# A top-k attention and two gated expert layers on one core: the first batch in plain float32, score tiles copied out of PSUM

## The chip, the core and the metric

The kernel runs on one core of one Trainium2 chip. The metric is the device time of one execution in microseconds (us). The engines are TensorE (PE in the profile, its weight loads PEld), VectorE (DVE), ScalarE (ACT), GpSimd (POOL) and SyncE (SP), whose queue issues all of this kernel's DMAs. TensorE writes only PSUM, a memory of eight banks of 512 float32 columns; all else lies in SBUF.

## The reference

Attention over 4 batches, 8 heads, 576 positions and head size 64, in which each query keeps its 32 best scores, then two expert layers on the 2304 tokens:

```python
scores = scale * np.matmul(q, k.transpose(0, 1, 3, 2))
kth = np.partition(scores, -32, axis=-1)[..., -32:-31]
scores = np.where(scores >= kth, scores, -1e9)
attn = softmax(scores)                               # rows of 576
x = (attn @ v) as 2304 x 512                         # float32
h = x @ w_in;  g = where(h >= 1, h, where(h <= -1, 0, (h + 1)**2 / 4));  x = g @ w_out     # 512 -> 2048 -> 512
g = x @ w_gate;  out = (g * sigmoid(g) * (x @ w_val)) @ w_out2                             # 512 -> 1536 -> 512
```

The weights come in as 8-byte floats, and the attention scores must be near float32, since a wrong score changes which 32 are kept.

## The kernel before

**Arithmetic.** Nearly all matmuls take float32r, a 4-byte form of which one pass does not carry all float32 digits. So each operand is split into a high and a low part (`split`, `hilo`: ACT writes the high part, POOL subtracts for the low one), and a product is made of three or four matmuls. Transposes of the attention weights are plain float32 (`L747`, `L751`).

**Attention.** A unit is one batch, a pair of heads and a block of query tiles (two tiles of 128, or three of which the last holds 64 rows of each head). There are 8 units per batch, first block before second block, and 36 score tiles of 128 x 576 in each batch, 144 in all. For each score tile PE writes two half rows of 288 columns into one of two pairs of PSUM banks, `pS` (`L672`, four matmuls; each pair holds one score tile). DVE then works on it for some 6 us: four times MAX8 (`L686`), three times MATCH_REPLACE8 (`L696`) between them, and one SCALAR_TENSOR_TENSOR, the mask (`L700`), which compares the scores with the 32nd, multiplies with the exponentials that ACT has made (`L693`) and sums. The first MAX8, the first MATCH_REPLACE8, the exponential and the mask read the scores in PSUM, so a pair of banks comes free with the mask. Then PE transposes the masked tile (`L747`), ACT takes it out as high part (`L732`) and full copy (`L734`), POOL subtracts the low part (`L736`), PE multiplies with v (`L615`, `L617`), two ACT copies and two POOL operations add the parts and divide by the sum. In the 8 units of batch 0 (`LO_PE = 8`) the low part comes from PE instead: it subtracts the high part in PSUM with a matmul by a negative identity (`L725`), and ACT copies both parts (`L723`, `L727`).

**Preparing q, k, v.** Each is loaded per head pair, split by ACT and POOL (`L482`, `L484`), and q and k are transposed by PE and taken out by ACT (`L501`, `L537`).

**Weights.** 68 tiles of 8-byte weights are turned into high and low float32r by ACT (`L827`, `L830`, `L837`), DVE (`L832`) and POOL (`L835`, `L850`) and stored in DRAM. In the first 24, DVE's `L832` reads one operand in PSUM (a `pM` bank), in the other 44 both in SBUF.

**Expert layers.** `STEPS` goes through the tokens in subsets of 256 (the last one 512), first layer 1 (`L967`, `L1009`), then layer 2 (`L967`, `L1081`). Their sums lie in `pM`, two PSUM banks while attention runs; the other six are `pS` (four) and `pT` (two, transposes and attention outputs). When all attention is done, `pS` and `pT` pass to the experts (`p.heirs`).

**Order.** A planner (`Plan`) runs a list schedule forward and backward over all operations, with a price for each and the sizes of the rings of buffers, and writes one fixed order per engine. Each engine then does its instructions in that order, and waits at each for what it needs.

## Time and profile before

| what | value |
|---|---|
| median of 3 runs | 1330.06 us (1329.61 to 1332.45) |
| profiled execution, span from first to last instruction | 1326.2 us |
| busy: PE / DVE / ACT / POOL | 1208.5 / 1017.7 / 876.4 / 778.3 us |
| mean granted TensorE clock | 0.957 of full |

The profile is of one execution, and its page gives for that only the span; the median lies 3.9 us above it. In the page's 40 slices each digit is a tenth of busy time in 33 us. "Busy" of PE counts a matmul from its start to its modelled end, so neighbours overlap. The group rows give the mean duration of one instruction in ns, then the idle time of its engine just ahead of it and what ended that.

### The profile page before, as it was taken

How to read it: one execution, taken by the hardware profiler on the slowest of the kernel's cores; microseconds unless marked ns; L12 is line 12 of the kernel's file. 1: busy time of each engine (PE TensorE's matmuls, PEld its weight loads, DVE VectorE, ACT ScalarE, POOL GpSimd, SP SyncE). 2: the span in 40 equal slices, each digit the busy share in tenths (PEclk: the TensorE clock that was granted, in tenths of full speed). 3: DMA queues.
4: the chain of work that ended last, by engine and by line, in shares of the span. 5: the costliest groups of instructions: out<-in, count | busy, mean ns of one | idle time of the engine just before them, and what ended most of it. 6: DMA issues, size and time to landing. Idle time of an engine off the chain costs nothing.

```text
span 1326.2 us, 23321 instructions
## 1 busy us (share of the span) xinstructions
PE 1208.5 (91%) x7832; PEld 1095.6 (83%) x7832; DVE 1017.7 (77%) x2066; ACT 876.4 (66%) x1926; POOL 778.3 (59%) x831
## 2 busy tenths in 40 slices
PE   2556589888899999999999999999999999999998
PEld 2444489886799989998999988889999888888887
DVE  5899999899899989999999898989999312212212
ACT  6889799889777578776879777767766322333220
POOL 7888868689856465866667665556655313213210
PEclk9666699999899999999999999999999999999999
DMA  8788879789877786778676854548666754666452
GB/s 279 276 287 272 287 262 350 280 269 337 294 272 280 276 320 240 297 263 304 232 275 227 318 196 128 176 162 288 216 252 249 283 198 146 248 220 220 163 191 64
DMA packets 137032, 328.18 MB, mean 247 GB/s; under 512 B 21072, under 2 KB 66640, under 8 KB 136912
## 3 DMA queue, kind: packets, MB, share of 16 engines
q1 hardware_dynamic: 136912, 326.68, 70.2%
q8 instruction: 62, 1.02, 0.3%
q14 instruction: 58, 0.48, 0.1%
HBM read 282.07 MB, written 44.56 MB: 246 GB/s over the span
## 4 chain that ended last, share of the span: by engine, by line
PE 68%; DMA 9%; ACT 7%; DVE 7%; POOL 6%; issue 3%; SPq 0%; DVEq 0%; POOLq 0%; ACTq 0%
PE pM L967 25%; PE pM L1009 10%; PE pM L1081 7%; PE late L967 7%; PE pS L672 4%; PE pT L615 4%; PE late L1081 3%; PE pT L747 3%; DVE v L686 2%; PE late L1009 2%; DVE R L696 2%; POOL ct L835 2%; DMA cv<-in_moe_w_val_dram 2%; DMA cv<-in_moe_w_out_dram 1%; DMA w<-ws_moe_w_out 1%
## 5 line engine op out<-in xcount | busy, mean ns | idle before, releaser
L686 DVE MAX8 v<-R 128x8 f32<-128x576 f32 x432 | 315.1, 749 | 0.8
L967 PE MATMUL pM<-w,w 128*128 128x256 f32 (+1 forms) x1719 | 295.8, 319 | 3.5 <-DVE t L1105 2.5
L967 PEld LDWEIGHTS pM<-w,w 128*128 128x128 f32 x1719 | 249.9, 196 | 19.7 <-DVE t L1105 2.6
L736 POOL TENSOR_TENSOR PT<-F,PT 128x384 fp32r<-128x384 f32 (+2 forms) x192 | 176.7, 930 | 90.8 <-ACT F L734 84.4
L875 POOL TENSOR_TENSOR w<-t,w 128x512 fp32r<-128x512 f32 x110 | 142.2, 1295 | 135.1 <-ACT w L873 113.8
L696 DVE MATCH_REPLACE8 R<-v,R 128x576 f32<-128x576 f32 x288 | 213.8, 743 | 0.0
L686 DVE MAX8 v<-pS 128x8 f32<-128x576 f32 x144 | 109.3, 759 | 38.8 <-PE pS L672 36.3
L1009 PE MATMUL pM<-w,w 128*128 128x256 f32 (+1 forms) x867 | 132.2, 291 | 1.3 <-DVE t L1047 1.3
L693 ACT ACTIVATE E<-pS,nb 128x576 f32<-128x576 f32 x144 | 107.4, 746 | 25.3 <-DVE R L696 19.2
L747 PE MATMUL pT<-idf,E 128*128 128x128 f32 x512 | 95.9, 293 | 28.9 <-ACT qT L537 16.0
L1009 PEld LDWEIGHTS pM<-w,w 128*128 128x128 f32 x867 | 114.2, 190 | 4.0 <-DVE t L1047 2.7
L672 PE MATMUL pS<-kT,qT 128*128 128x288 f32 x512 | 100.9, 321 | 17.2 <-DVE E L700 14.9
L700 DVE SCALAR_TENSOR_TENSOR E<-pS,v,E 128x576 f32<-128x576 f32 x144 | 115.8, 804 | 0.2
L732 ACT ACTIVATE PT<-pT 128x384 fp32r<-128x384 f32 (+2 forms) x192 | 88.4, 463 | 40.6 <-PE pT L747 21.6
L696 DVE MATCH_REPLACE8 R<-v,pS 128x576 f32<-128x576 f32 x144 | 107.7, 748 | 0.0
L873 ACT ACTIVATE w<-t 128x512 fp32r<-128x512 f32 x110 | 70.5, 642 | 54.0 <-DVE t L1115 43.0
L835 POOL TENSOR_TENSOR ct<-ct,cv 128x512 int32<-128x512 int32 x68 | 91.4, 1348 | 22.9 <-ACT ct L830 15.1
L875 POOL TENSOR_TENSOR late<-t,late 128x512 fp32r<-128x512 f32 x32 | 41.3, 1293 | 103.8 <-ACT late L873 84.1
L747 PEld LDWEIGHTS pT<-idf,E 128*128 128x128 f32 x512 | 65.3, 148 | 42.6 <-ACT qT L537 18.1
L672 PEld LDWEIGHTS pS<-kT,qT 128*128 128x128 f32 x512 | 82.1, 206 | 22.3 <-DVE E L700 17.6
L967 PE MATMUL pM<-late,w 128*128 128x256 f32 (+1 forms) x597 | 98.5, 302 | 0.7 <-DVE t L1047 0.6
L615 PE MATMUL pT<-PT,v 128*128 128x256 f32 (+1 forms) x512 | 94.1, 310 | 3.9 <-ACT PT L727 3.1
(138 smaller groups left out, 2679.7 us busy)
## 6 DMA issues: line engine op xcount, KB each, us to landing
w<-ws_moe_w_out SPq DMA_DIRECT2D x134, 512.0 KB, 6.3
w<-ws_moe_w_in SPq DMA_DIRECT2D x90, 512.0 KB, 5.7
w<-ws_moe_w_val SPq DMA_DIRECT2D x55, 512.0 KB, 5.4
...
```

The source lines that it names most:

```text
L615: nc.tensor.matmul(av[:, 0:N], V[:, h, c, :], PT[:, s, h * 4 + c, 0:N], start=s == 0 and c == 0, stop=False)
L672: nc.tensor.matmul(ps[:, j, 0:288], l(), kT[:, hh, at + j * 288:at + (j + 1) * 288], start=k == 0, stop=k == len(lhs) - 1)
L686: p.op("DVE", self.dve(576) + (0 if k else self.PS), lambda: nc.vector.max(out=v8[:, h, k, :], in_=rr() if k else sc()), [Rb if k else ps] ...
L696: p.op("DVE", self.dve(576) + 0.06 + (0 if k else self.PS), lambda h=h, k=k, sc=sc, rr=rr: nc.vector.match_replace(out=rr(), in_to_replace ...
L700: p.op("DVE", self.dve(576) + 0.06 + self.PS, lambda h=h, sc=sc, ee=ee: nc.vector.scalar_tensor_tensor(out=ee(), in0=sc(), scalar=v8[:, h, ...
L736: p.op("POOL", self.pool(n), lambda: nc.gpsimd.tensor_tensor(out=dst(1), in0=src(F), in1=dst(0).bitcast(F32), op=OP.subtract), [F, (PT, (0 ...
L747: fn = (lambda ps=ps, m=m, h=h, c=c: nc.tensor.transpose(ps[:, m * 128:(m + 1) * 128], Sb[:, h, 64 * h + c * 128:64 * h + (c + 1) * 128], ...
L835: p.op("POOL", self.pool(512), lambda: nc.gpsimd.tensor_tensor(out=ci(), in0=ci(), in1=word(0), op=OP.add), [(cv, 0)], [ct], 3, tag + "cvadd")
L875: p.op("POOL", self.pool(n), lambda: nc.gpsimd.tensor_tensor(out=dst[:, 1, to:to + n], in0=src[:, off:off + n], in1=dst[:, 0, to:to + n].b ...
L967: nc.tensor.matmul(ps[:, at:at + n], W[:, w, k * 128:(k + 1) * 128], x[:, s, xat:xat + n], start=k == 0 and j == 0, stop=k == KC - 1 and j ...
L1009: nc.tensor.matmul(ps[:, at:at + n], WO[f][:, v, j * 128:(j + 1) * 128], g[:, s, gat:gat + n], start=q == 0 and m == 0, stop=q == 3 and m ...
L1081: nc.tensor.matmul(ps[:], a[:, s, at:at + 128], WO[f][:, v, :], start=q == 0 and m == 0, stop=q == 3 and m == 2)
```

## The change

Batch 0 is computed without splitting: `load_raw0` puts the two heads of a pair side by side, one transpose gives both stacked on 128 partitions, scores and outputs are plain float32 matmuls (`prep_k32`, `prep_q32`, `prep_v32`), and the attention weights are copied once. In all batches ACT copies each score tile from PSUM to SBUF (`C`, two buffers), and DVE and the exponential read `C`. `pS` shrinks to one pair of banks and `pM` grows from two banks to four. Buffers of batch 0 (`kF`, `vF`, `qF`, `PF`, `raw0`) pass on to the later batches (`chain`) in a fixed sequence. `E` has two buffers instead of three. A few prices of the planner change (`DMA_LAT`, ACT on converts and on copies across partitions, POOL), and switches that no longer choose anything go (`LO_W`, `QFIRST`, `AV_POOL`, `LATE`, `BANKS`). The core of the diff:

```diff
-    DMA_LAT = 1.7
+    DMA_LAT = 2.0
...
-    LO_PE = 8
+    FIRST_B = 1
...
-        self.r_v = R("v", [128, 2, 5, 2 * D], F32R, self.KV)
+        self.r_raw0 = R("raw0", [128, 5, 2 * D], F32, 2)
+        self.r_hl = R("hl", [128, 2, 5, 2 * D], F32R, 0)
+        self.r_v = R("v", [128, 2, 5, 2 * D], F32R, 0)
...
-        self.r_qT = R("qT", [128, 2, 2, 256], F32R, self.QT)
+        self.r_qT = R("qT", [128, 2, 2, 256], F32R, 0)
...
-        self.r_kT = R("kT", [128, 2, 640], F32R, self.KV)
-        self.r_E = R("E", [128, 2, S], F32, 3)
+        self.r_kT = R("kT", [128, 2, 640], F32R, 0)
+
+        self.r_kF = [R("kF%d" % i, [128, 2, 640], F32, 1) for i in range(HP)]
+        self.r_vF = [R("vF%d" % i, [128, 10, 128], F32, 1) for i in range(HP)]
+        self.r_qF = R("qF", [128, 512], F32, 2)
+        self.r_PF = R("PF", [128, 9, 320], F32, 2)
+        self.r_E = R("E", [128, 2, S], F32, 2)
...
-        self.r_PT = R("PT", [128, 2, 9, 320], F32R, 1)
+        self.r_PT = R("PT", [128, 2, 9, 320], F32R, 0)
...
-        self.p_s = R("pS", [128, 2, 512], F32, 2, "P")
+        self.p_s = R("pS", [128, 2, 512], F32, 1, "P")
+        self.r_C = R("C", [128, S], F32, 2)
         self.p_t = R("pT", [128, 512], F32, self.PT_BANKS, "P")
-        self.p_m = R("pM", [128, 512], F32, 4 - self.PT_BANKS, "P")
-
-        p.heirs = [((self.r_cv, self.r_ct), self.r_w, 5)] * self.LATE
-
-        p.heirs += [((self.p_s, self.p_t), self.p_m, 4 + self.PT_BANKS)] * self.BANKS
+        self.p_m = R("pM", [128, 512], F32, 6 - self.PT_BANKS, "P")
+
+        self.chain = []
+        for i in range(HP):
+            self.chain += [((self.r_kF[i],), self.r_kT, 1), ((self.r_vF[i],), self.r_v, 1)]
+        self.chain[-1:] = [((self.r_raw0,), self.r_hl, 1), ((self.r_qF,), self.r_qT, 1), self.chain[-1],
+                           ((self.r_PF,), self.r_PT, 1), ((self.r_cv, self.r_ct), self.r_w, 5)]
+        gone = ()
+        for own, ring, n in self.chain:
+            gone += own
+            p.heirs.append((gone, ring, n))
+        self.chain.append(((self.p_s, self.p_t), self.p_m, 2 + self.PT_BANKS))
+        p.heirs.append(self.chain[-1])
...
             self.p.rush = self.FIRST and u == 0
+            if b < self.FIRST_B:
+                if blk == 0:
+                    kF = self.prep_k32(b, hp)
+                state["q", u] = self.prep_q32(b, hp, self.BLOCKS[b][blk])
+                self.p.rush = False
+                if blk == 0:
+                    state["kv", b, hp] = kF, self.prep_v32(b, hp)
+                return
...
+    def load_raw0(self, src, b, hp, a=0, z=5):
+
+        raw = self.r_raw0.new()
+        m = min(z, 4)
+        for h in (0, 1):
+            d = slice(64 * h, 64 * h + 64)
+            if m > a:
+                self.dma(lambda d=d: raw[:, a:m, d],
+                         lambda h=h: src[b, 2 * hp + h, 0:512, :].rearrange("(p c) d -> p c d", c=4)[:, a:m, :],
+                         128 * 256 * (m - a), writes=[(raw, h)], prio=2, tag="ldqkv")
+            if z == 5:
+                self.dma(lambda d=d: raw[d, 4, d], lambda h=h: src[b, 2 * hp + h, 512:576, :],
+                         32 * 1024, writes=[(raw, 2 + h)], prio=2, tag="ldqkv")
+        return raw
+
+    def prep_k32(self, b, hp):
+
+        nc, p = self.nc, self.p
+        kF = self.r_kF[hp].new()
+        raw = self.load_raw0(self.t["k"], b, hp)
+        ps = self.p_t.new()
+        for c in range(4):
+            p.op("PE", 0.11, lambda c=c: nc.tensor.transpose(ps[:, c * 128:(c + 1) * 128], raw[:, c, :], self.idf),
+                 [raw], [(ps, c)], 1, "kTt")
+        p.op("ACT", self.act(512), lambda: nc.scalar.activation(
+            out=kF[:, 0, 0:512], in_=ps[:], func=AF.Copy), [ps], [(kF, 0)], 2, "kTe")
+        pl = self.p_t.new()
+        p.op("PE", 0.11, lambda: nc.tensor.transpose(pl[:, 0:128], raw[:, 4, :], self.idf), [raw], [pl], 1, "kTt")
+        for h, r in enumerate((slice(0, 64), slice(64, 128))):
+            p.op("ACT", self.act(64), lambda r=r: nc.scalar.activation(
+                out=kF[r, 0, 512:576], in_=pl[r, r], func=AF.Copy), [pl], [(kF, 1 + h)], 2, "kTe")
+        return kF
+
+    def prep_v32(self, b, hp):
+
+        p, t = self.p, self.t["v"]
+        vF = self.r_vF[hp].new()
+        nc = self.nc
+        p.op("DVE", self.dve(1280), lambda: nc.vector.memset(vF[:], 0.0), [], [vF], 1, "vz")
+        for h in (0, 1):
+            d = slice(64 * h, 64 * h + 64)
+            self.dma(lambda h=h, d=d: vF[:, 4 * h:4 * h + 4, d],
+                     lambda h=h: t[b, 2 * hp + h, 0:512, :].rearrange("(p c) d -> p c d", c=4),
+                     128 * 1024, writes=[(vF, h)], prio=2, tag="ldqkv")
+            self.dma(lambda d=d: vF[d, 8, d], lambda h=h: t[b, 2 * hp + h, 512:576, :],
+                     32 * 1024, writes=[(vF, 2 + h)], prio=2, tag="ldqkv")
+        return vF
+
+    def prep_q32(self, b, hp, qts):
+
+        nc, p = self.nc, self.p
+        raw = self.load_raw0(self.t["q"], b, hp, qts[0], qts[-1] + 1)
+        qF = self.r_qF.new()
+        ps = self.p_t.new()
+        n = len(qts) * 128
+        for i, c in enumerate(qts):
+            p.op("PE", 0.11, lambda i=i, c=c: nc.tensor.transpose(ps[:, i * 128:(i + 1) * 128], raw[:, c, :], self.idf),
+                 [raw], [(ps, i)], 1, "qTt")
+        p.op("ACT", self.act(n), lambda: nc.scalar.activation(
+            out=qF[:, 0:n], in_=ps[:, 0:n], func=AF.Copy), [ps], [qF], 2, "qTe")
+        return qF
...
+        plain = b < self.FIRST_B
+        if plain:
+            av = self.p_t.new()
+
+            def mms():
+                for s in range(9):
+                    nc.tensor.matmul(av[:, 0:N], V[:, s, :], PT[:, s, 0:N], start=s == 0, stop=s == 8)
+            p.op("PE", self.mm(4 * N, 9), mms, [V] + [(PT, (i, g)) for i, t in enumerate(qts) for g in ((0, 1, 2) if t < 4 else ("a", ("b", 0), ("b", 1)))], [av], 1, "av")
+            p.op("ACT", self.act(N), lambda: nc.scalar.activation(
+                out=y[:, 0:N], in_=av[:, 0:N], func=AF.Copy), [av], [y], 2, "ave")
+        else:
+            tmp = self.r_tmp.new()
...
+            if plain:
+                cols = slice(i * 128, (i + 1) * 128)
+                r = slice(64 * h, 64 * h + 64) if t < 4 else slice(0, 128)
+                parts = ((0, 0, 0, 288), (1, 0, 288, 576)) if t == 4 or h == 0 else ((0, 0, 512, 576), (0, 64, 0, 224), (1, 0, 224, 512))
+                rd = [q] + [(kT, e) for e in (0, 1, 2)]
...
+                if plain:
+                    mine = [x for x in parts if x[0] == j]
+
+                    def mms(ps=ps, mine=mine, r=r, cols=cols):
+                        for jj, at, a, z in mine:
+                            nc.tensor.matmul(ps[:, jj, at:at + z - a], q[r, cols], kT[r, 0, a:z], start=True, stop=True)
+                    p.op("PE", sum(self.mm(4 * (z - a)) for _, _, a, z in mine), mms, rd, [(ps, j)], 0, "qk")
+                    continue
...
-            def vmax(k, h=h, ps=ps, Rb=Rb, sc=sc, rr=rr):
-                p.op("DVE", self.dve(576) + (0 if k else self.PS), lambda: nc.vector.max(
-                    out=v8[:, h, k, :], in_=rr() if k else sc()), [Rb if k else ps], [(v8, (h, k))], 6, "max8")
+            Cb = self.r_C.new()
+
+            def cc(Cb=Cb):
+                return Cb[:].rearrange("p (j n) -> p j n", j=2)
+            p.op("ACT", self.act(576), lambda sc=sc, cc=cc: nc.scalar.activation(out=cc(), in_=sc(), func=AF.Copy), [ps], [Cb], 1, "scp")
+            def vmax(k, h=h, Cb=Cb, Rb=Rb, cc=cc, rr=rr):
+                p.op("DVE", self.dve(576), lambda: nc.vector.max(
+                    out=v8[:, h, k, :], in_=rr() if k else cc()), [Rb if k else Cb], [(v8, (h, k))], 6, "max8")
 
...
-            p.op("ACT", self.act(576, self.FN - self.SB), lambda h=h, sc=sc, ee=ee: nc.scalar.activation(
-                out=ee(), in_=sc(), func=AF.Exp, bias=nb[:, h:h + 1], scale=0.125), [ps, (nb, h)], [(Eb, h)], 1, "exp")
+            p.op("ACT", self.act(576, self.FN), lambda h=h, cc=cc, ee=ee: nc.scalar.activation(
+                out=ee(), in_=cc(), func=AF.Exp, bias=nb[:, h:h + 1], scale=0.125), [Cb, (nb, h)], [(Eb, h)], 1, "exp")
             for k in range(3):
-                p.op("DVE", self.dve(576) + 0.06 + (0 if k else self.PS), lambda h=h, k=k, sc=sc, rr=rr: nc.vector.match_replace(
-                    out=rr(), in_to_replace=v8[:, h, k, :], in_values=rr() if k else sc(), imm_value=NEG),
-                    ([] if k else [ps]) + [(v8, (h, k))], [Rb], 6, "mrep")
+                p.op("DVE", self.dve(576) + 0.06, lambda h=h, k=k, cc=cc, rr=rr: nc.vector.match_replace(
+                    out=rr(), in_to_replace=v8[:, h, k, :], in_values=rr() if k else cc(), imm_value=NEG),
+                    ([] if k else [Cb]) + [(v8, (h, k))], [Rb], 6, "mrep")
                 vmax(k + 1)
-            p.op("DVE", self.dve(576) + 0.06 + self.PS, lambda h=h, sc=sc, ee=ee: nc.vector.scalar_tensor_tensor(
-                out=ee(), in0=sc(), scalar=v8[:, h, 3, 7:8], in1=ee(),
+            p.op("DVE", self.dve(576) + 0.06, lambda h=h, cc=cc, ee=ee: nc.vector.scalar_tensor_tensor(
+                out=ee(), in0=cc(), scalar=v8[:, h, 3, 7:8], in1=ee(),
                 op0=OP.is_ge, op1=OP.mult, accum_out=rs[:, i, h:h + 1]),
-                [ps, (v8, (h, 3))], [(Eb, h), (rs, (i, h))], 5, "mask")
+                [Cb, (v8, (h, 3))], [(Eb, h), (rs, (i, h))], 5, "mask")
...
-            if lo_pe and key in range(3):
-
-                p.op("ACT", self.act(n), lambda: nc.scalar.activation(out=dst(0), in_=src(ps), func=AF.Copy),
-                     [ps], [(PT, (0, i, key))], 2, "PThi")
-                p.op("PE", self.mm(n), lambda: nc.tensor.matmul(
-                    src(ps), self.idn[:], dst(0), start=False, stop=True, skip_group_check=True), [(PT, (0, i, key))], [(ps, None)], 1, "PTn")
-                p.op("ACT", self.act(n), lambda: nc.scalar.activation(out=dst(1), in_=src(ps), func=AF.Copy),
-                     [ps], [(PT, (1, i, key))], 2, "PTlo")
+            if plain:
+                p.op("ACT", self.act(n), lambda: nc.scalar.activation(out=dst(None), in_=src(ps), func=AF.Copy),
+                     [ps], [(PT, (i, key))], 2, "PThi")
```

The places that matter below, as the engines' instruction orders have them. First ACT at the very start of the program, in which `cv` are loaded weights, `ct`, `w` and `pM` their converted pieces, `kT`/`kF` and `qF` the transposed keys and queries, and `C` the new copy; before:

```order
L482 ACTIVATE hq_190<-raw_184 128x2x2x64
L827 ACTIVATE pM_253<-cv_243 128x512
L482 ACTIVATE hl_185<-raw_183 128x10x64
L830 ACTIVATE ct_247<-cv_243 128x512
L827 ACTIVATE pM_254<-cv_244 128x512
L1196 ACTIVATE idn<-idf 128x128
L830 ACTIVATE ct_248<-cv_244 128x512
L827 ACTIVATE pM_253<-cv_245 128x512
L501 ACTIVATE kT_193<-pT_251 128x512
```

and now:

```order
L935 ACTIVATE ct_280<-cv_276 128x512
L932 ACTIVATE pM_288<-cv_277 128x512
L935 ACTIVATE ct_281<-cv_277 128x512
L558 ACTIVATE kF_220<-pT_285 128x512
L932 ACTIVATE pM_289<-cv_278 128x512
L563 ACTIVATE kF_220<-pT_286 64x64 x2
L942 ACTIVATE w_254<-ct_280 128x512
L592 ACTIVATE qF_228<-pT_285 128x256
L932 ACTIVATE pM_290<-cv_279 128x512
L942 ACTIVATE w_255<-ct_281 128x512
L935 ACTIVATE ct_280<-cv_278 128x512
L792 ACTIVATE C_283<-pS_282 128x576
```

The splits are gone, the first transposed keys are taken out at the sixth place of ACT's order (counted from its table load) instead of the tenth, and the first copy of a score tile stands behind the first step of four weight tiles' conversions.

Next PE at the end of attention: the last transposes of an attention tile (`E`), the expert matmuls around them (`pM<-`, 512 columns, three passes each), and the first attention outputs behind them; before:

```order
L747 MATMUL pT_252<-idf,E_198 128x128 x3
L747 MATMUL pT_251<-idf,E_198 128x128 x3
L967 MATMUL pM_254<-w_235,late_1_3206 128x512 x3
L967 MATMUL pM_253<-w_235,w_227 128x512 x3
L747 MATMUL pT_252<-idf,E_198 128x128 x2
L751 MATMUL pT_252<-idf,E_198 128x128
L967 MATMUL pM_254<-w_233,late_1_3206 128x512 x3
L967 MATMUL pM_253<-w_233,w_227 128x512 x3
L967 MATMUL pM_254<-w_234,late_1_3206 128x512 x3
L615 MATMUL pT_251<-PT_215,v_189 128x256 x4
```

and now:

```order
L1060 MATMUL pM_287<-w_265,w_267 128x512 x3
L1060 MATMUL pM_288<-w_268,late_2_2879 128x512 x3
L1060 MATMUL pM_288<-late_3_2880,late_2_2879 128x512 x3
L852 MATMUL pT_285<-idf,E_233 128x128 x2
L852 MATMUL pT_286<-idf,E_233 128x128 x2
L856 MATMUL pT_286<-idf,E_233 128x128
L1060 MATMUL pM_288<-w_262,late_2_2879 128x512 x3
L1060 MATMUL pM_288<-w_265,late_2_2879 128x512 x3
L1060 MATMUL pM_289<-w_268,w_259 128x512 x3
L1060 MATMUL pM_289<-late_3_2880,w_259 128x512 x3
L707 MATMUL pT_285<-late_0_2791,late_0_2786 128x256 x4
```

What moved is how far the experts have come at that point. Counted to the end of PE's order, 1242 expert matmuls of 512 columns stand behind the last transposes before (762 of `L967`, 192 of `L1009`, 288 of `L1081`), and 1194 now (714, 192 and 288); the 20 attention outputs and 2 transposes left are the same.

## Rows read from the trace of the kernel before

**Rows 1.** Page, 40 slices of 33 us: busy tenths, and granted clock.

```profile
PE   2556589888899999999999999999999999999998
DVE  5899999899899989999999898989999312212212
PEclk9666699999899999999999999999999999999999
```

**Rows 2.** Four stretches: length, busy us (instructions) of PE, PEld, DVE, ACT, POOL; clock, DMA.

```profile
0.00:166.00 166.00, 85.54 (x367) 67.52 (x368) 138.57 (x275) 136.82 (x281) 135.52 (x137) 0.70 0.82 280
166.00:400.00 234.00, 209.24 (x1542) 196.35 (x1541) 219.56 (x443) 199.98 (x443) 182.67 (x181) 0.97 0.84 294
400.00:1040.00 640.00, 631.73 (x4676) 598.24 (x4675) 596.29 (x1258) 467.33 (x1082) 395.74 (x463) 1.00 0.71 251
1040.00:1326.00 286.00, 281.99 (x1254) 233.48 (x1252) 63.32 (x92) 72.25 (x122) 64.35 (x52) 1.00 0.53 183
```

**Rows 3.** Waits of DVE, 33 to 1034 us: total us, times, longest us.

```profile
DVE v L686 <- PE pS L672: 36.3, 57, 1.8
DVE cv L832 <- ACT pM L827: 5.6, 6, 1.9
```

**Rows 4.** Timeline of the start: start us, us, engine, line, operation.

```profile
7.04 0.72 ACT L482 ACTIVATE hl<-raw 128x640 fp32r<-128x640 f32 x1
7.84 1.53 POOL L484 TENSOR_TENSOR hl<-raw,hl 128x640 fp32r<-128x640 f32 x1 [2.65 <-DVE cv L832]
...
9.43 1.26 PE L498 MATMUL pT<-idr,hl 128*128 128x128 f32 x8 [9.43 <-POOL hl L484]
...
18.26 0.76 DVE L686 MAX8 v<-pS 128x8 f32<-128x576 f32 x1
```

**Rows 5.** Groups by line and shape: busy us, mean ns, idle before.

```profile
L686 DVE MAX8 v<-R 128x8 f32<-128x576 f32 x432 | 315.1, 749 | 0.8
L696 DVE MATCH_REPLACE8 R<-v,R 128x576 f32<-128x576 f32 x288 | 213.8, 743 | 0.0
L700 DVE SCALAR_TENSOR_TENSOR E<-pS,v,E 128x576 f32<-128x576 f32 x144 | 115.8, 804 | 0.2
L686 DVE MAX8 v<-pS 128x8 f32<-128x576 f32 x144 | 109.3, 759 | 38.8 <-PE pS L672 36.3 <-PE pT L747 1.4 <-PE pT L544 0.5
L696 DVE MATCH_REPLACE8 R<-v,pS 128x576 f32<-128x576 f32 x144 | 107.7, 748 | 0.0
L832 DVE SCALAR_TENSOR_TENSOR cv<-cv 128x512 int32<-128x512 int32 x44 | 43.1, 980 | 4.5 <-ACT cv L827 3.0 <-issue 1.4
L887 ACT ACTIVATE t<-pM 128x512 f32<-128x512 f32 x50 | 30.1, 602 | 17.4 <-PE pM L1081 9.4 <-PE pM L1009 7.6
L725 PE MATMUL pT<-PT,idn 128*128 128x384 f32 x48 | 22.9, 488 | 13.5 <-ACT PT L723 13.5
L832 DVE SCALAR_TENSOR_TENSOR cv<-cv,pM 128x512 int32<-128x512 int32 x24 | 16.5, 685 | 22.0 <-ACT pM L827 21.1 <-issue 0.9
```

**Rows 6.** Line L832 with both operands in SBUF: duration ns min/median/max, first and last start.

```profile
L832 DVE SCALAR_TENSOR_TENSOR cv<-cv x44: 669/822/1798, 102.1 to 319.3; 128x512 int32<-128x512 int32 x44
```

**Rows 7.** The stretch of those 44, columns as in Rows 2.

```profile
102.00:320.00 218.00, 174.61 (x1173) 158.70 (x1173) 207.45 (x404) 190.77 (x417) 176.28 (x168) 0.88 0.84 292
```

**Rows 8.** Timeline around the last score tile's mask and the last transposes.

```profile
1032.85 0.81 DVE L700 SCALAR_TENSOR_TENSOR E<-pS,v,E 128x576 f32<-128x576 f32 x1
...
1037.49 0.27 PE L751 MATMUL pT<-idf,E 128*128 128x128 f32 x1
...
1042.37 9.10 PE L967 MATMUL pM<-w,w 128*128 128x512 f32 x39
```

**Rows 9.** Timeline, 500 to 520 us: five float32 transposes in a row.

```profile
507.64 0.57 PEld L747 LDWEIGHTS pT<-idf,E 128*128 128x128 f32 x5
```

More of the change, by code (lines that the diff above doesn't have):

```diff
@@ L564, in queries @@
                 ahead()
-            later = lambda t=t, i=i, Eb=Eb: self.transposes(t, i, Eb, unit["PT"], lo_pe)
+            later = lambda t=t, i=i, Eb=Eb: self.transposes(t, i, Eb, unit["PT"], plain)
         later()
@@ L1153, in emit @@
             pools[z] = stacks[z].enter_context(tc.tile_pool(name=f"first{z}", bufs=1, **space))
[L1154 to L1155 removed]
+            still[z] = sum(r.count for r in own)
+            passing.update({id(r): z for r in own})
         for r in p.rings:
```

117 lines of the change are left out of this document (52 added, 65 removed).

## The prediction

> **What bounds the kernel now.** I read the page's slices first, then the busy time by stretch, the waits of the engine that looked full, and the timeline where something has to start or end. In the slices DVE stands at 8 or 9 tenths until about slice 31 and then falls to 1 to 3, while PE climbs from half to full and stays there; its granted clock is about 6 tenths, so mostly the lower of its levels, while it is half idle early on [rows 1]. By stretch: to 166 us PE is busy for 85.5 of 166 us and DVE for 138.6; from 166 to 400 us PE for 209.2 of 234 and DVE for 219.6; from 400 to 1040 us 631.7 and 596.3 of 640; behind that PE is full and DVE nearly empty [rows 2]. So the span has two parts. Until the last score tile is masked at 1032.85 us and transposed at 1037.49 [rows 8], DVE sets the pace in the first third and shares it with PE later. Then PE alone works off what is left, which sets the end. The time is the moment of the last transposes plus the PE work that stands behind them. I work out both, in the profiled execution: span 1326.2 us, 3.9 below the median; I assume that gap stays.
>
> **The start (A).** The first MAX8 starts at 18.26 us. On its path lie ACT's split of k at 7.04, POOL's subtraction of 1.53 us behind it, and transposes only at 9.43 [rows 4]. Both split steps go, some 2.4 us, as do two ACT copies of the rearranged queries. Against that the loads of k and q come in six DMAs instead of four, issued one after the other by SP, and ACT's order puts steps that wait for the third and fourth weight tile ahead of the first copy of scores. Four memsets of v tiles stand at the head of DVE's order, where it idles. I take -3 us, bounds -6 and +3.
>
> **DVE's work for a score tile (B).** Nothing leaves DVE's list, only its operands move from PSUM to SBUF. The rows show both cases for MAX8, 759 ns from PSUM and 749 from SBUF, and for MATCH_REPLACE8, 748 and 743 [rows 5]; I give the mask 16 ns, since `L832`'s shortest with both operands in SBUF is 669 ns against a mean of 685 with one in PSUM [rows 5, 6]. That is 31 ns by 144 tiles, -4.5 us.
>
> The mask is the other side. It now reads two operands in SBUF, the copied scores and the exponentials. The trace has one operation in both forms: `L832` takes 685 ns with one operand in PSUM and 980 with both in SBUF, and it is not a constant price: shortest 669, median 822, longest 1798 [rows 5, 6]. Its 44 cases lie where POOL is busy for 176.3 of 218 us, 0.81 [rows 7], so the excess of 295 ns is about 365 ns by POOL's share. The Trainium skill, "SBUF — State Buffer", section "Who interferes with whom", gives the reason: DVE's second SBUF input comes through an interface that it shares with GpSimd, and whoever comes second waits for the other's whole instruction. The trace agrees: a median of 822 under a longest of 1798 is a wait, not a slower rate. By that rule every mask is exposed; without it the mask would only gain its 16 ns.
>
> In the changed kernel POOL loses batch 0's splits and low parts of outputs, so I take a share of 0.75 for batch 0's 36 masks: 36 x 0.27 = 9.9 us. For the other 108 its share is 395.7 of 640 us, 0.62 [rows 2]: 108 x 0.226 = 24.4 us. Together +34.3; bounds 0 and 144 x 0.295 = 42.5. B is +30 us, bounds -5 and +38.
>
> **DVE's idle time (C).** From 33 to 1034 us DVE waited 36.3 us in 57 pieces for PE to write the next scores [rows 3], because the pair of banks came free only with the mask and PE then had to get to it. Now a third score tile lies ready in `pS` while two are worked on in `C`. What is late next is the copy: when a mask frees its `C`, ACT must copy 576 columns. The nearest row is 602 ns for 512 from PSUM [rows 5], so about 655 ns, and behind whatever ACT has in hand. ACT is busy for 467 of 640 us [rows 2], and the 108 copies of batches 1 to 3 add about 71, so such a wait is short and rarer. I take 22 of the 36 us back, bounds 0 and 36. `L832`'s 5.6 us of waiting for ACT [rows 3] should halve, since ACT loses in each unit of batch 0 the splits, the second copies of the weights and the swapped copies of q: -3. C is -25 us, bounds -39 and 0.
>
> The copies take nothing from DVE's own list and lie beside it. If ACT were full, each would cost DVE its 0.65 us, up to 94 us over 144; at 0.73 + 0.11 of ACT's time it is not.
>
> **What is left for PE (D).** Between the last transposes and the end of the span lie 1326.2 - 1037.8 = 288.4 us for 1242 matmuls of 512 columns and a few small ones; a run of 39 takes 9.10 us, 0.233 each [rows 8]. The changed order leaves 1194: 48 x 0.233 = -11 us. These 48 were moved ahead of the last transposes, where PE must find time for them. PE's idle time by busy share is 24.8 us from 166 to 400 and 8.3 to 1040 [rows 2], and the longer score queue and four expert banks are what lets them in. Bounds -11, and 0 if they delay the transposes by as much.
>
> **PE's work in batch 0.** It loses 92,160 columns of float32r scores and outputs and the 48 identity matmuls `L725` (22.9 us busy, overlapping) [rows 5], and gains 41,472 columns of plain float32. No row shows a float32 product. Its lower bound is the float32r pace, 233/512 = 0.455 ns a column [rows 8]; the nearest row above is the float32 transpose, five of 128 columns in 0.57 us, 0.89 ns a column [rows 9]. That makes 19 to 37 us against 42 before, so a gain of 5 to 23 us of PE time, of which nearly half falls before 166 us, where PE idles for 80 us anyway. I count 0 for the end. The Trainium skill, "FP8 and Floating Point Precision", section "TensorE Precision Notes", says that true FP32 takes four passes; by that these columns would cost about 76 us, 34 more than before, and no run here shows it. It is the third rival.
>
> **The sum.** A -3, B +30, C -25: the last transposes come 2 us later. D -11. Span 1326.2 - 9 = 1317.2, and with 3.9 around it about 1321 us. With each term's error the case's own range is 1308 to 1332.
>
> **The rivals.**
>
> 1. *The mask's wait for POOL decides (slower).* Place: the mask row, on DVE, all 144 tiles. Each pays the whole 295 ns, and ACT's copy takes the place of PE's scores as what DVE waits for, so C is only -3: -3 + 38 - 3 - 11 = +21, 1351 us. It decides from where B eats A, C and D, 39 us with my C: 39/144 + 31 = 302 ns, a mean of the mask row of about 1.09 us; with C at -3 already from 0.93 us. For it: DVE has only 44 of 640 us free in the middle stretch, and the orders are fixed. Against it: POOL is less busy there than where the 295 were seen.
>
> 2. *The coupling loosens more (faster).* All 36 us come back, the mask waits 150 ns because DVE and POOL settle beside each other: B (150 - 31) x 144 = 17, C -39, A -3, D -11: -36, 1294 us. For it: a deeper queue and twice the expert banks meet engines that are both nearly full. Against it: ACT's copies are in-order work, and PE is idle for only 33 us after 166.
>
> 3. *PE becomes the bound in batch 0 (no gain).* Batch 0's second block, for which PE also has the first expert work, holds 23,040 of the float32 columns, in place of 53,248 of float32r and 24 identity matmuls. If a float32 column costs four times a float32r one, 1.82 ns, that is 42 us for 24, and less about 4 for the identities +14 in a stretch where PE idles for 24.8 [rows 2]. If none of that idle time can take it, the sum is -9 + 14 = +5, 1335 us. The skill's rule of four passes, named above, is what would make it so. For it: the slices show PE at 8 to 9 tenths there [rows 1]. Against it: the idle time.
>
> **How the numbers follow.** My forecast 0.42, rival 1 (with its milder forms) 0.27, rival 2 0.17, rival 3 0.14. 0.2%, or 2.7 us, is about what can be told from no change here. Of the forecast's 0.42 about 0.36 is faster and 0.05 the same; rival 2 is all faster; rival 3 is 0.05 faster, 0.04 same, 0.05 slower; rival 1 slower but for 0.01. So faster 0.58, same 0.10, slower 0.32. For 8 in 10 the range goes to rival 2's middle and nearly to rival 1's full price: 1297 to 1346.
>
> **What would show it.** A: first MAX8 near 15 us. B: a mask row of mean about 1.02 us, with a shortest near 0.79. C: DVE's waits for the next scores, now for the ACT copy, near 14 us in total. The last transposes near 1040 us and some 277 us behind them. PE: the rows of the plain score and output matmuls give the float32 pace. I am wrong in B if the mask's mean is under 0.85 or over 1.1, in C if the waits for the copy exceed 30 us, in D if the stretch behind the last transposes is not shorter, and rival 3 is right if PE is full between 166 and 300 us while DVE waits for it.

## The result, and the profile after

| | before | changed | ratio |
|---|---|---|---|
| median of 4 runs each, us | 1331.26 | 1308.41 | 0.9836, 95% interval [0.9813, 0.9858] |
| lowest to highest, us | 1329.61 to 1333.39 | 1306.07 to 1310.15 | |

The kernel became 1.6% faster. The direction was forecast and the time lies in the range, but 12.6 us below the forecast of 1321. The profiled execution took 1309.97 us with a span of 1308.2, so 18.0 us less span than before. The medians lie 22.9 us apart: the median lies 5.1 us above the profiled span before and 0.2 above it after, so about 5 us of the gain are in no row of the two profiles.

Slices of PE, DVE and the granted clock, to be laid beside [rows 1]:

```profile
PE   3566799998999999999999999999999999999998
DVE  6989999999999999999999999999999512222212
PEclk9967699999999999999999999999999999999999
```

PE reaches 9 tenths in the sixth slice, and DVE has no 8 left between the fourth slice and the end of its part. The first three stretches of [rows 2], cut at the same times, with the same columns:

```profile
0.00:166.00 166.00, 102.99 (x341) 69.97 (x342) 142.54 (x275) 115.98 (x223) 114.60 (x116) 0.79 0.83 269
166.00:400.00 234.00, 221.41 (x1559) 197.96 (x1559) 232.28 (x438) 194.96 (x404) 193.63 (x169) 0.99 0.90 320
400.00:1040.00 640.00, 637.43 (x4684) 604.32 (x4684) 621.29 (x1274) 521.35 (x1185) 422.23 (x466) 1.00 0.70 250
```

From 166 to 400 us PE idled for 24.8 us and now for 12.6; DVE for 14.4 and now for 1.7. The start, as in [rows 4]:

```profile
9.02 1.09 PE L556 MATMUL pT<-idf,raw 128*128 128x128 f32 x4 [9.02 <-DMA raw<-in_k_dram]
...
15.12 0.65 ACT L792 ACTIVATE C<-pS 128x576 f32<-128x576 f32 x1 [0.73 <-PE pS L769]
15.81 0.76 DVE L794 MAX8 v<-C 128x8 f32<-128x576 f32 x1 [1.81 <-ACT C L792]
```

The transposes of k now wait for the load itself, no longer for a split, and start 0.41 us earlier; behind them another 2 us are won, so the first MAX8 starts 2.45 us earlier. DVE's groups, as in [rows 5], then the mask and the conversion line by duration, as in [rows 6] (ns min/median/max):

```profile
L808 DVE SCALAR_TENSOR_TENSOR E<-C,v,E 128x576 f32<-128x576 f32 x144 | 157.7, 1095 | 0.1
L794 DVE MAX8 v<-C 128x8 f32<-128x576 f32 x144 | 107.4, 746 | 14.8 <-ACT C L792 13.8 <-POOL nb L798 0.3 <-POOL late L503 0.3
L804 DVE MATCH_REPLACE8 R<-v,C 128x576 f32<-128x576 f32 x144 | 106.5, 740 | 0.0
```

```profile
L808 DVE SCALAR_TENSOR_TENSOR E<-C,v,E x144: 789/942/1901, 27.8 to 1026.7; 128x576 f32<-128x576 f32 x144
...
L937 DVE SCALAR_TENSOR_TENSOR cv<-cv x44: 667/740/1865, 108.3 to 321.7; 128x512 int32<-128x512 int32 x44
L937 DVE SCALAR_TENSOR_TENSOR cv<-cv,pM x24: 666/687/699, 7.4 to 101.3; 128x512 int32<-128x512 int32 x24
```

The mask's shortest is below its old mean of 804 ns, its longest is more than twice as long, and 144 of them take 157.7 us (mean 1095 ns) in place of 115.8. `L937` is the control in the same profile: its longest is 699 ns while one operand is in PSUM, and 1865 once both are in SBUF. DVE's waits from its first MAX8 to the last transposes (us, times, longest), beside [rows 3]:

```profile
DVE v L794 <- ACT C L792: 13.8, 17, 3.0
DVE cv L937 <- ACT pM L932: 5.8, 7, 2.2
DVE cv L937 <- issue: 2.3, 3, 1.5
DVE cv L937 <- ACT cv L932: 2.0, 3, 1.3
```

The end, as in [rows 8], and PE behind it (length, busy us, instructions):

```profile
1026.74 1.09 DVE L808 SCALAR_TENSOR_TENSOR E<-C,v,E 128x576 f32<-128x576 f32 x1
...
1030.40 0.27 PE L856 MATMUL pT<-idf,E 128*128 128x128 f32 x1
```

```profile
1030.67:1308.00 277.33, 273.37 (x1217) 1.00 0.52 178
```

The last transposes end at 1030.67, 7.1 us earlier than before (2 later was forecast), and 277.5 us of span follow (277 was forecast; before 288.4).

### The profile page after: what moved, and what is told of

It is laid out like the page before. It is cut to its first block, busy times and chain, and to the rows that moved or that the text cites. A ratio compares the mean times of both kernels' runs of the same rounds, so it can differ in the third digit from the quotient of the medians.

```text
span 1308.2 us, 23150 instructions
## 1 busy us (share of the span) xinstructions
PE 1225.9 (94%) x7744; PEld 1090.6 (83%) x7744; DVE 1054.9 (81%) x2070; ACT 898.6 (69%) x1921; POOL 790.0 (60%) x797
## 4 chain that ended last, share of the span: by engine, by line
PE 68%; DMA 11%; DVE 10%; ACT 4%; issue 3%; POOL 3%; SPq 1%; POOLq 0%; DVEq 0%; ACTq 0%
PE pM L1060 27%; PE pM L1102 9%; PE pM L1174 8%; PE late L1060 5%; PE pS L775 4%; PE pT L707 4%; DVE v L794 4%; DVE R L804 3%; PE pT L852 3%; PE late L1174 2%; PE late L1102 2%; DMA cv<-in_moe_w_out_dram 2%; DMA ws_moe_w_out<-cv 2%; DMA cv<-in_moe_w_in_dram 1%; DVE E L808 1%
## 5 line engine op out<-in xcount | busy, mean ns | idle before, releaser
L841 POOL TENSOR_TENSOR late<-F,late 128x384 fp32r<-128x384 f32 (+1 forms) x180 | 179.4, 1008 | 61.9 <-ACT F L839 53.6
L808 DVE SCALAR_TENSOR_TENSOR E<-C,v,E 128x576 f32<-128x576 f32 x144 | 157.7, 1095 | 0.1
L792 ACT ACTIVATE C<-pS 128x576 f32<-128x576 f32 x144 | 94.0, 653 | 43.8 <-DVE E L808 37.7
L801 ACT ACTIVATE E<-C,nb 128x576 f32<-128x576 f32 x144 | 112.6, 783 | 15.4 <-POOL nb L798 14.7
L794 DVE MAX8 v<-C 128x8 f32<-128x576 f32 x144 | 107.4, 746 | 14.8 <-ACT C L792 13.8
L940 POOL TENSOR_TENSOR ct<-ct,cv 128x512 int32<-128x512 int32 x68 | 92.5, 1362 | 43.0 <-DVE cv L937 12.9
L852 PEld LDWEIGHTS pT<-idf,E 128*128 128x128 f32 x512 | 65.1, 148 | 58.1 <-DVE E L808 29.1
L967 ACT ACTIVATE w<-t 128x512 fp32r<-128x512 f32 x106 | 67.1, 635 | 59.2 <-DVE t L1208 52.6
L804 DVE MATCH_REPLACE8 R<-v,C 128x576 f32<-128x576 f32 x144 | 106.5, 740 | 0.0
L837 ACT ACTIVATE late<-pT 128x384 fp32r<-128x384 f32 (+1 forms) x180 | 84.9, 472 | 14.2 <-PE pT L865 4.7
L1060 PEld LDWEIGHTS pM<-late,w 128*128 128x128 f32 x618 | 86.9, 190 | 4.9 <-POOL late L969 0.2
L1174 PE MATMUL pM<-w,w 128*128 128x512 f32 x324 | 88.8, 405 | 0.7 <-POOL w L944 0.6
L1060 PE MATMUL pM<-w,late 128*128 128x256 f32 (+1 forms) x456 | 86.1, 325 | 0.0
```

What stands on the lines that cost most here:

```text
L792: p.op("ACT", self.act(576), lambda sc=sc, cc=cc: nc.scalar.activation(out=cc(), in_=sc(), func=AF.Copy), [ps], [Cb], 1, "scp")
L794: p.op("DVE", self.dve(576), lambda: nc.vector.max(out=v8[:, h, k, :], in_=rr() if k else cc()), [Rb if k else Cb], [(v8, (h, k))], 6, "max8")
L801: p.op("ACT", self.act(576, self.FN), lambda h=h, cc=cc, ee=ee: nc.scalar.activation(out=ee(), in_=cc(), func=AF.Exp, bias=nb[:, h:h + 1], ...
L804: p.op("DVE", self.dve(576) + 0.06, lambda h=h, k=k, cc=cc, rr=rr: nc.vector.match_replace(out=rr(), in_to_replace=v8[:, h, k, :], in_valu ...
L808: p.op("DVE", self.dve(576) + 0.06, lambda h=h, cc=cc, ee=ee: nc.vector.scalar_tensor_tensor(out=ee(), in0=cc(), scalar=v8[:, h, 3, 7:8], ...
L841: p.op("POOL", self.pool(n), lambda: nc.gpsimd.tensor_tensor(out=dst(1), in0=src(F), in1=dst(0).bitcast(F32), op=OP.subtract), [F, (PT, (0 ...
```

## The experiments

Two theories stood at first. **Theory 1**: the copy frees the score banks early, and DVE's regained idle time is the whole gain. **Theory 2**: the copy only pays, and plain float32 in batch 0 brings the gain. **Theory 3** came with them: the planner's new prices, for which the forecast had no term, bring it through the order. Each run was timed beside the kernel before, whose median was 1329.5 to 1330.6 us on these chips. Intervals are those of the ratio to it.

**e1, the copy and the banks alone; e2, plain float32 alone**

```diff
 e1, on the kernel before
-        self.r_E = R("E", [128, 2, S], F32, 3)
+        self.r_E = R("E", [128, 2, S], F32, 2)
...
-        self.p_s = R("pS", [128, 2, 512], F32, 2, "P")
+        self.p_s = R("pS", [128, 2, 512], F32, 1, "P")
+        self.r_C = R("C", [128, S], F32, 2)
...
-        self.p_m = R("pM", [128, 512], F32, 4 - self.PT_BANKS, "P")
+        self.p_m = R("pM", [128, 512], F32, 6 - self.PT_BANKS, "P")
... (ACT's copy into C; DVE and the exponential read C)
 e2, on the changed kernel: the reverse, but E keeps two buffers
```

> The kernel before, with only the score copy taken over: two tiles C in SBUF, one pair of score banks, four expert banks until the scores are done, two tiles E. Batch 0 keeps its split float32r and the prices stay. Theory 1 (the copy frees the score banks early, and that gives DVE its idle time back): DVE's idle time between first and last mask falls from about 66 us to 35 or less, the mask row rises to about 1.05 us, the last transposes come within 5 us of 1037 and the time is 1315 to 1328 us. Theory 2 (the copy only pays: what was won came from batch 0 in plain float32, which unloads ACT and POOL and gives PE its work sooner): idle time stays above 50 us, the mask's 35 us are lost, and the time is 1340 us or more.

> The changed kernel without the score copy: DVE and the exponential read the scores in PSUM as in the kernel before, two pairs of score banks, two expert banks; batch 0 in plain float32, the chain of freed tiles and the new prices stay. Theory 1 (the copy does it): mask row at 0.80 us again, the waits for the next scores at 30 us or more again, time 1318 to 1330 us. Theory 2 (batch 0 in plain float32 does it): idle time as low as in the changed kernel, and without the mask's 42 us the time is under 1300 us.

Measured: e1 1334.97 us, ratio 1.0038 [1.0026, 1.0050]; e2 1324.74 us, 0.9960 [0.9948, 0.9972]. First e1's rows, then e2's:

```profile
L706 DVE SCALAR_TENSOR_TENSOR E<-C,v,E 128x576 f32<-128x576 f32 x144 | 158.0, 1097 | 0.9 <-ACT E L699 0.6
L692 DVE MAX8 v<-C 128x8 f32<-128x576 f32 x144 | 107.8, 749 | 22.5 <-ACT C L690 20.7 <-POOL PT L742 1.1 <-ACT rs L715 0.3
```

```profile
L802 DVE SCALAR_TENSOR_TENSOR E<-pS,v,E 128x576 f32<-128x576 f32 x144 | 115.9, 805 | 0.4
L788 DVE MAX8 v<-pS 128x8 f32<-128x576 f32 x144 | 109.6, 761 | 51.8 <-PE pS L774 27.8 <-PE pS L768 14.4 <-POOL y L718 2.3
```

Theory 1 is right on the idle time: with the copy alone it falls from 65.4 us to 34.9, without it it stays at 69.0. It is not shown that this is a gain by itself: e1's mask takes 42 us more, and the time, 4.4 us above the kernel before, lies between the forecasts of both theories. Theory 2 falls: with plain float32 alone the idle time stays and the time is far from 1300. Both differences, e1's and e2's, are smaller than what another order of the same instructions makes (below). PE behind the last transposes, of the kernel before, e1 and e2 (length, busy us, instructions):

```profile
1037.76:1326.00 288.24, 284.23 (x1265) 1.00 0.53 185
```

```profile
1051.19:1332.00 280.81, 276.70 (x1232) 1.00 0.51 178
```

```profile
1034.38:1321.40 287.02, 282.89 (x1259) 1.00 0.52 182
```

So most of the shorter end comes with the copy and its banks, not with plain float32. The spans of e1 and e2 differ from the kernel before by +5.8 and -4.8 us, +1.0 together, and the changed kernel by -18.0: what the two halves bring only together stays open, and it is no more than the orders' spread. No run separates the third `E` buffer or the fixed sequence of freed buffers.

**e3 and e4, the prices changed alone**

```diff
 e3, on the changed kernel (e4: the reverse, on the kernel before)
-    DMA_LAT = 2.0
+    DMA_LAT = 1.7
...
-    CVX, XP = 0.045, 0.125
+    CVX, XP = 0.0, 0.0
...
-        return 0.149 + n * 0.00215
+        return 0.149 + n * 0.0021
...
-        rate = 310e3 if tag.endswith("ldw64") and narrow else Plan.DMA_RATE
+        rate = Plan.DMA_RATE
```

> The changed kernel planned with the prices of the kernel before (DMA latency 1.7, no extra for the conversions and the swapped copies, one DMA rate, POOL 2.1 ns an element). Only the order of the instructions differs. If the order by the new prices is what brought the extra 11 us (theory 3): 1317 us or more. If not (theories 1 and 2): 1304 to 1313 us.

> The kernel before planned with the new prices, nothing else. Theory 3 (the prices): 1320 us or less. Theories 1 and 2: within 5 us of the kernel before, 1326 to 1336 us.

Measured: e3 1319.05 us, 0.9917 [0.9897, 0.9937]; e4 1322.93 us, 0.9947 [0.9929, 0.9965]. The order moves the time by 11 us in the one kernel and by 8 in the other. Whether that is a price's worth or any order's chance was the next question.

**e9 to e12, one price at a time**

```diff
 e9
-    DMA_LAT = 2.0
+    DMA_LAT = 1.7
...
-        rate = 310e3 if tag.endswith("ldw64") and narrow else Plan.DMA_RATE
+        rate = Plan.DMA_RATE
 e10
-    CVX, XP = 0.045, 0.125
+    CVX, XP = 0.0, 0.0
 e11
-        return 0.149 + n * 0.00215
+        return 0.149 + n * 0.0021
 e12
-    DMA_LAT = 2.0
+    DMA_LAT = 2.3
```

> The changed kernel planned with the old DMA latency and the one DMA rate; the other new prices stay. Theory 3a (one of the new prices tells the planner something true, and the 10.6 us are its worth): either this run or the next carries 7 us or more of it (1315 us or more here) and the other two of these runs stay within 3 us of the changed kernel. Theory 3b (any other price gives another order, and orders spread by some 10 us with no price to be named): all four runs lie above the changed kernel, by 3 to 14 us, the meaningless one too.

> The changed kernel planned without the extra price of ACT's conversions and swapped copies (0.045 and 0.125 us); the other new prices stay. Theory 3a: 1315 us or more here if it isn't the DMA price, else 1305 to 1311. Theory 3b: 1311 to 1322.

> The changed kernel planned with POOL at 2.10 ns an element in place of 2.15, 26 ns of 1.2 us in an instruction. Theory 3a: too small to matter, 1305 to 1311 us. Theory 3b: 1311 to 1322.

> The changed kernel planned with a DMA latency of 2.3 in place of 2.0 us, a step further the same way. Theory 3a: if the latency is what counts, the planner only allows more, 1304 to 1311 us. Theory 3b: 1311 to 1322.

Measured: 1328.16 [0.9959, 0.9999], 1316.35 [0.9872, 0.9916], 1317.98 [0.9870, 0.9922] and 1314.22 us [0.9860, 0.9894]. Theory 3b: all four are slower than the changed kernel, by 6 to 20 us (it gave 3 to 14), also for a price that differs by 26 ns in an instruction. e9, which keeps the new prices of the conversions and of POOL, is even slower than e3, which keeps none.

**e13, e14, e16: is the kernel before an ordinary one of its orders, and does a true price help?**

```diff
 e13, on the kernel before
-    DMA_LAT = 1.7
+    DMA_LAT = 2.0
 e14, on the kernel before
-        return 0.149 + n * 0.0021
+        return 0.149 + n * 0.00215
 e16, on the changed kernel
-    SB, FN, PS, PORT = 0.043, 0.136, 0.065, 0.0
+    SB, FN, PS, PORT = 0.043, 0.136, 0.065, 0.29
...
-            p.op("DVE", self.dve(576) + 0.06, lambda h=h, cc=cc, ee=ee: ...
+            p.op("DVE", self.dve(576) + 0.35, lambda h=h, cc=cc, ee=ee: ...
```

> The kernel before planned with a DMA latency of 2.0 in place of 1.7 us. If the kernel before is an ordinary one of its orders: 1322 to 1338 us, on either side of it. If it is a poor one, and the change of design brought less than it seems: 1324 us or less, as with all new prices (1322.9).

> The kernel before planned with POOL at 2.15 ns an element in place of 2.10. The same question: an ordinary order gives 1322 to 1338, a poor one 1324 or less here too.

> The changed kernel planned with the mask and the conversions in SBUF each 0.29 us longer, as measured. If orders are a matter of chance: 1311 to 1325 us like the other four. If a true price helps the planner: 1308 us or less.

Measured: e13 1341.57 us [1.0077, 1.0125], e14 1329.46 [0.9987, 1.0019], e16 1329.43 [0.9989, 1.0018]. The kernel before is an ordinary one of its orders. e13 and e16 lie some 4 us above the ranges expected of them. Telling the planner the mask's measured wait gave one of the two slowest orders of the seven. All orders side by side, from the timelines and windows of their profiles; the median is of all executions, the other columns are of the profiled one, which lies up to 3.7 us off it (e9, whose executions run from 1320.9 to 1332.3). The idle time is counted from the first MAX8 to the start of the last mask:

| kernel, order | median us | first MAX8 | DVE busy to last mask | DVE idle to last mask | last transposes | span behind them |
|---|---|---|---|---|---|---|
| before | 1330.6 | 18.26 | 949.2 | 65.4 | 1037.8 | 288.4 |
| before, e4 | 1322.9 | 18.36 | 947.2 | 53.2 | 1022.8 | 296.5 |
| before, e13 | 1341.6 | 19.56 | 951.8 | 77.0 | 1052.6 | 287.7 |
| before, e14 | 1329.5 | 19.55 | 954.8 | 67.9 | 1044.8 | 286.4 |
| changed | 1308.4 | 15.81 | 984.5 | 26.4 | 1030.7 | 277.5 |
| changed, e3 | 1319.1 | 15.39 | 983.0 | 34.3 | 1037.6 | 280.9 |
| changed, e9 | 1328.2 | 15.45 | 982.5 | 34.3 | 1036.1 | 286.4 |
| changed, e10 | 1316.4 | 15.74 | 990.8 | 26.5 | 1039.6 | 278.2 |
| changed, e11 | 1318.0 | 15.41 | 984.4 | 29.5 | 1034.8 | 281.3 |
| changed, e12 | 1314.2 | 16.41 | 988.6 | 24.3 | 1033.2 | 278.2 |
| changed, e16 | 1329.4 | 16.26 | 994.8 | 45.3 | 1062.2 | 263.9 |

The mean is 1331.2 us over four orders of the kernel before and 1319.1 over seven of the changed one: 12 us. The other 10 are that the changed kernel runs in the best order of the seven. These are few orders, and not drawn at random, so 12 is an estimate: within each group the medians scatter by some 7.5 us, which leaves a standard error of about 5 us on it.

**e5, e15, e17, e18: what the freed banks are worth**

```diff
 e5 (e15: and DMA_LAT = 2.3)
-        self.p_m = R("pM", [128, 512], F32, 6 - self.PT_BANKS, "P")
+        self.p_m = R("pM", [128, 512], F32, 4 - self.PT_BANKS, "P")
...
-        self.chain.append(((self.p_s, self.p_t), self.p_m, 2 + self.PT_BANKS))
+        self.chain.append(((self.p_s, self.p_t), self.p_m, 4 + self.PT_BANKS))
 e17 (e18: 3)
-    PT_BANKS = 2
+    PT_BANKS = 1
```

> The changed kernel with two expert banks instead of four until the scores are done; two banks stay unused. It measures the four banks, and is the base for the next two runs. Theory DVE (the last transposes come when DVE's list is through, and DVE's idle time is what was won): DVE does not read those banks first, 1306 to 1311 us. Theory PE (the time is PE's own work plus its idle time before about 300 us, whatever DVE does later): with fewer banks PE gets less expert work in beside the scores, its idle time before 400 us rises by 4 us or more, 1312 to 1322 us.

> The changed kernel with two expert banks, planned with a DMA latency of 2.3 us. If the banks carry the 43 us: 1340 to 1358 us, against 1314.2 for four banks at this price. If it was the order: under 1335 us.

> The changed kernel with one bank for the transposes and the outputs of attention instead of two, and five expert banks instead of four. If PE's expert work is still held up by banks at four: fewer matmuls left behind the last transposes (under 1200) and 1290 to 1306 us. If four is enough: nothing gained there, and each transpose group must now wait for ACT to empty the one bank before the next can be written; the last transposes come 10 us later or more, 1325 us or more.

> The changed kernel with three banks for the transposes and three expert banks. If each expert bank carries some 20 us: 1328 to 1342 us, with 1290 to 1350 matmuls behind the last transposes. If the loss lies in having two alone: within the spread of orders of four banks, 1308 to 1328 us.

Measured: e5 1351.15 us [1.0125, 1.0189], e15 1355.33 [1.0174, 1.0239], e17 1420.26 [1.0666, 1.0710], e18 1321.10 [0.9912, 0.9958]. PE behind the last transposes, of e5, of e18 and of e17:

```profile
1042.12:1349.00 306.88, 303.01 (x1415) 1.00 0.56 202
```

```profile
1035.97:1315.00 279.03, 275.40 (x1226) 1.00 0.50 178
```

```profile
1159.32 0.27 PE L856 MATMUL pT<-idf,E 128*128 128x128 f32 x1
1159.59:1416.00 256.41, 252.30 (x1123) 1.00 0.52 183
```

Two expert banks cost 43 us against four (41 in the other order): 198 more matmuls are left for the end, and of e5's 41 us of span 30 lie behind the last transposes and 11 ahead of them. Both theories had put e5 at 1322 us or less. Three banks are enough beside a third transposes' bank, which e18 has too: it lies among the orders with four. A fifth, at the price of a transposes' bank, leaves fewer matmuls for the end, 1123, but is a loss of 112 us: DVE's waits for the copy rise to 61.8 us, and the last transposes end at 1159.6, 129 us later. Beside e2, which has two expert banks too but two pairs of score banks and no copy, e5 is 26 us slower, more than orders of one kernel lie apart here. So the copy is worth taking only with the banks that it frees. One thing stays open: PE's records in e5 hold 1246.3 us in place of 1225.9 for as many instructions, 7744. The mean granted clock is 0.961 there and 0.972 in the changed kernel, so part of the 20 us can be matmuls at the lower clock; no run separates that.

**e6, e7, e8: DVE's list or PE's work?**

```diff
 e6, on e5, batch 0 alone (e7, batches 1 to 3 alone: direct = not plain)
+        self.p_e = R("pE", [128, 2, 512], F32, 1, "P")
...
+            direct = plain
+            Xb = self.p_e.new() if direct else (Eb, h)
...
-                out=ee(), in_=cc(), func=AF.Exp, ...
+                out=xx(), in_=cc(), func=AF.Exp, ...
...
-                out=ee(), in0=cc(), scalar=v8[:, h, 3, 7:8], in1=ee(),
+                out=ee(), in0=cc(), scalar=v8[:, h, 3, 7:8], in1=xx(),
 e8, on the changed kernel
-    FIRST_B = 1
+    FIRST_B = 2
```

> As the run with two expert banks, but the exponentials of batch 0 go to a pair of PSUM banks, so that batch 0's 36 masks read one operand in SBUF and one in PSUM. Their row falls from about 1.19 us to 0.80, which takes some 14 us off DVE's list, all before about 250 us, where PE still idles. Theory PE: half of that or more reaches the end, -5 to -14 us against the run with two banks. Theory DVE: -14 us against that run.

> As the run with two expert banks, but the exponentials of batches 1 to 3 go to the pair of PSUM banks. 108 masks fall from about 1.06 us to 0.80, some 28 us off DVE's list, nearly all behind 250 us, where PE is full. Theory DVE: the last transposes and the end come 15 to 28 us earlier. Theory PE: PE has nothing more to give there, the last transposes come earlier but the stretch behind them grows by as much; within 5 us of the run with two banks.

> The changed kernel with batch 1 in plain float32 too. PE's work grows as it did for batch 0, by about 20 us, now in a stretch where PE is full, while ACT and POOL lose batch 1's splits and the second copies. Theory PE: 12 to 22 us slower than the changed kernel, 1320 to 1332 us. Theory DVE: DVE's list keeps its length and POOL gets less in its way, 1300 to 1311 us.

Measured: e6 1343.54 us [1.0065, 1.0106], e7 1335.84 [1.0029, 1.0065], e8 1355.31 [1.0167, 1.0205]. The mask in e7:

```profile
L814 DVE SCALAR_TENSOR_TENSOR E<-C,v,pE x108: 775/802/816, 311.2 to 1025.8; 128x576 f32<-128x576 f32 x108
```

With one operand in PSUM the wait is gone from all 108: a median of 802 ns and a longest of 816. The masks together take 152.7 us in e5, 142.9 in e6 and 129.9 in e7, so DVE is spared 9.8 and 22.8 us, less than the 14 and 28 expected. The time falls by 7.6 and 15.3 us: the last transposes come 7.9 and 12.9 us earlier, and the span behind them, 307.5 us in e5, is 307.8 and 304.9. That it does not grow speaks against theory PE, and neither run shows the whole of DVE's relief in the time. But these are single orders, and other orders move the time by as much; what share reaches the end is not shown. Then the same edit as for batch 0, made to batch 1, PE's totals of the changed kernel and then of e8:

```profile
PE 1225.9 (94%) x7744; PEld 1090.6 (83%) x7744; DVE 1054.9 (81%) x2070; ACT 898.6 (69%) x1921; POOL 790.0 (60%) x797
```

```profile
PE 1267.3 (94%) x7704; PEld 1104.7 (82%) x7704; DVE 1052.4 (78%) x2074; ACT 844.9 (62%) x1773; POOL 704.2 (52%) x713
```

PE is busy for 41 us more and the time rises by 47 (theory PE said 12 to 22), though ACT and POOL lose 54 and 86 us of work. The span outside PE's busy time is 85 us, as in the changed kernel's 82: there PE has no idle time for it.

## Why the prediction was right in direction and wrong in size

| term, us of span | forecast | in this order | mean of orders |
|---|---|---|---|
| A, start | -3 | -2.5 | -3.2 |
| B, DVE's work | +30 | +35.3 | +36.2 |
| C, DVE's idle time | -25 | -39.0 | -34.4 |
| last mask to last transposes | 0 | -1.0 | +1.0 |
| D, PE behind them | -11 | -10.9 | -11.7 |
| sum | -9 | -18.0 | -12.1 |

The orders' column is the difference of the two groups' means in the table of orders. Of the 12.6 us between the forecast and the median, 9 are in this sum. The rest is the distance from the span to the median, which I assumed to stay at 3.9 us and which was 0.2; the four executions alone lie up to 4.1 us apart.

- **A and D** were right to a microsecond. In A most of the split's 2.4 us was lost again, as the load of k lands only at 9.02 us. e1 and e5 show on what D hangs: the copy with its expert banks.
- **B** was mis-sized by 5, the mask in it by 10: 41.9 us more, where the forecast had 32. I took a mean mask of 1.02 us from the price of 295 ns weighted with POOL's share; it was 1.095. The mask of batch 0 and of batches 1 to 3, then POOL in the same two stretches (length, busy us, and behind it clock and DMA):

```profile
L808 DVE SCALAR_TENSOR_TENSOR E<-C,v,E 128x576 f32<-128x576 f32 x36 | 42.8, 1189 | 0.0
L808 DVE SCALAR_TENSOR_TENSOR E<-C,v,E 128x576 f32<-128x576 f32 x108 | 114.9, 1064 | 0.1
```

```profile
27.00:312.00 285.00, 220.74 (x192) 0.87 0.88 299
312.00:1028.00 716.00, 490.65 (x533) 1.00 0.74 262
```

  Over the shortest of 789 ns that is 400 ns where POOL is busy for 0.77 of the time and 275 where it is for 0.69. So the wait does fall with POOL's share, as the weighting had it, but at some 515 and 400 ns by full share in place of 365, and I had taken 0.62 for the later share. That the wait hangs on both operands being in SBUF is shown by e7's row and by e6, whose 36 masks with one operand in PSUM took 789 to 812 ns; that POOL is the other side is argued from its share and from the rule that follows, and no run tests it. The Trainium skill, "SBUF — State Buffer", section "Who interferes with whom", says that DVE's second SBUF input and GpSimd share an interface; by that rule every mask was exposed, and the trace agrees, with 789 to 1901 ns. **Rival 1** thus had its price nearly right: the mean reached the 1.09 us from which it was to decide with my C. It fell because C was larger.
- **C is the step that failed.** Its first part came out: the wait for the next scores fell from 36.3 us to 13.8, by 22.5, where I took 22 back. That it came out so closely is partly luck: over the four and seven orders it falls from a mean of 34.6 us to 16.9. The second part did not: for all DVE's other waits I took 3 us. They were 29.1 of the 65.4 us of idle time, and 12.6 are left. The view of [rows 3] has them, from 18 us on, in the kernel before:

```profile
DVE cv L832 <- ACT pM L827: 10.3, 9, 3.0
DVE t L1047 <- ACT t L1045: 3.3, 5, 1.3
DVE cv L832 <- ACT cv L827: 3.0, 5, 1.0
DVE t L1115 <- PE pM L967: 3.0, 6, 1.0
DVE rc L712 <- ACT rs L709: 2.7, 3, 1.7
```

  In the changed kernel the conversion's two waits for ACT are 5.8 and 2.0 us, and the other three rows' successors wait for 0.4 us at most. In the mean of orders these other waits fall by as much, from 31.3 to 14.6 us, so it is not a matter of this order; C comes to -34.4 there, and the last 5 us belong to this order. My reason, that ACT is relieved of batch 0's splits, is not what brings it. e1 keeps the splits, and its two rows are

```profile
DVE cv L838 <- ACT cv L833: 2.7, 4, 1.3
DVE cv L838 <- ACT pM L833: 2.5, 3, 1.0
```

  with 14.2 us of other waits in all. In e2, without the copy, they stay at 26.8, and in e5, with the copy and two expert banks, at 26.4. These are single orders, but as they stand the fall comes with the banks that the copy frees. My signs of being wrong did not see it: the mask's mean stayed under 1.1 us and the waits for the copy under 30, and I had set no sign for DVE's other waits.
- **What the sum had no term for** is the order itself. I read one order before and one after as if a mechanism stood behind each place. Yet other orders of the same instructions take 6 to 21 us more, which is as large as most terms or larger. The forecast of 1321 us lies beside the orders' mean of 1319, though partly by luck, since B and C are off by 6 and 9 there in opposite directions; the 10 us to the measured time are the order's.
- **PE's work in batch 0**, counted as nothing, was outside its bounds (a gain of 5 to 23 us of PE time): e8's batch 1 costs PE 41 us more, net. The time was hardly touched: e2 and e4, which differ in the plain float32 and share the prices, lie 2 us apart. That PE's idle time took it up, 105.2 us in the first 400 before and 75.6 now, fits but is argued. The Trainium skill, "FP8 and Floating Point Precision", section "TensorE Precision Notes", speaks of four passes for true FP32, from which the prediction estimated 34 us for a batch; e8's 41 are near to it. **Rival 3** therefore had nearly the right price and the wrong place: made to batch 1, where PE has no idle time, the edit does cost time.
- **Rival 2** gave DVE's idle time right (-39) but had the mask settle at a wait of 150 ns. It didn't.
